# Pooled attention and two MoE layer pairs: another order in the prelude, and the second pair's first operands made in slots of the last token block

## The chip, the cores and the metric

The kernel runs on one core of a Trainium2 chip. The metric is device time in microseconds (us) of that core, as the median of several runs. The engines are TensorE (PE, with its weight loads as PEld), VectorE (DVE), ScalarE (ACT), GpSimd (POOL) and SyncE (SP, which here issues nearly all DMAs).

## The reference

Three stages follow each other on float inputs; weights and inputs of the two layer pairs arrive as float64.

```python
k_p = k.reshape(B, H, Sp, 8, D).mean(axis=3)      # B, H, S, D = 8, 8, 576, 64; Sp = 72
v_p = v.reshape(B, H, Sp, 8, D).mean(axis=3)
scores = scale * np.matmul(q, k_p.transpose(0, 1, 3, 2))
attn = np.exp(scores - np.max(scores, axis=-1, keepdims=True))
attn = attn / (np.sum(attn, axis=-1, keepdims=True) + 1e-09)
x = np.matmul(attn, v_p)                           # then (B*S, H*D) = 4608 x 512
y = ((x @ w_a) * (x @ w_b)) @ w_out                # w_a, w_b 512 x 1536
h = y @ w_in                                       # 512 x 2048
out = (h * np.clip(h + 3.0, 0.0, 6.0) / 6.0) @ w_out2
```

## The kernel before

**Attention.** The tokens are cut into chunks of up to 128, four of them (chunks 0 to 3) in the first block. For a batch, `k_dma` and `k_prep` load k and sum it in eights, `k_write` transposes it on PE (PSUM tile `ktp`) into the block matrix `bd`; `v_prep` and `v_write` make `vmh` and `vml` (the high part of v and the rest) for the first 64 pooled rows; `vl_dma`, `vl_prep`, `vl_split` and `vl_write` do it for the 8 left over (`vlraw`, `vls`, `vlhl`, `vlw`). For a chunk, `q_tr` transposes q (for batch 0 on PE, `qtp`), `scores` makes products `sc` and on DVE their maximum and difference (L263, L264), `expo` the exponential on ACT, `sums` the row sums on DVE (L279 to L283), `normal` the normalised weights on POOL, `at_main` and `at_left` their transposes (`atm`, `atl` on PE) with a split in high and low part (L330, L331, L341, L343), and `pv` the product with v, which fills the token block `xh`, `xl`.

**First layer pair.** There are nine blocks of 512 tokens (NB) and 12 slices of the inner width (NF1). `step(j, f)` makes `pa` and `pb` (from the block and a weight slice; in block 0 four matmuls of 512 columns each, which the trace shows as eight, and later twelve), copies them out on ACT (`asb`, `bsb`), multiplies them on POOL (L689), splits the product into `gh` and `gl`, and issues the `y` products of the step before (`y_part`, four banks), whose result `y_store` copies through the buffers `io` (two of them, tile `yo`) to `ydram`. In block 0 the weights are decoded from float64: `w1_begin` on ACT, `w1_mid` as two operations on DVE and one on POOL (L85 to L87), `w1_end` on DVE (L91), three parts to a slice, and products take one matmul per tile (L505, L519). From block 1 on each product is three matmuls (L497 to L499) of high and low parts.

**Order.** All of this stands in a manually scheduled stretch, in which every engine issues in the order of the code. `prelude()` is written out by hand: it does batch 0's attention for the first block and decodes the first weights. The rest of the attention is cut into pieces that `at(slot, ...)` puts into numbered slots, three to a step (36 to a block), which `run_slot` runs between `pa`, `pb` and `y`. `k_write` stands one slot behind `k_prep`.

**Second layer pair.** It stands behind the manual stretch, where the framework's scheduler picks the order on each engine and may put work ahead of the code's place. Two blocks make a super, and seven products per pair of slices (`in_prod`, banks `phZ`, `phW`, `phX`) work on sums of blocks and of weights. Their first operands are made by `y_load` (four tiles `yb` from `ydram`), `y_pre` (sums `T1`, `T2` and another, on POOL), `s_make` (seven pairs `Sh` on ACT and `Sl`, five of these on DVE and numbers 6 and 3 on POOL; number 4 begins with a sum on DVE), `w2_load` and `w2_make` (four weight sums on POOL, then splits `wi` and `wo` on ACT and DVE, of `wi` numbers 1 and 3 on POOL). A part of the results passes through `hs`, a tile of the same two `io` buffers. In the order that resulted, the first `phW` products stood in the middle of step 8's `y` products of the last block.

Of the kernel before, what the change touches and what calls it, by code (L numbers as in the profile page):

```python
# [8 lines left out]
F32 = mybir.dt.float32  # L9
# [16 lines left out]
def pooled_attention_then_two_moe_kernel(  # L26
# [371 lines left out]
    for c, (b, t0, n) in enumerate(chunks):  # L398
# [177 lines left out]
    def prelude():  # L576

        k_dma(0, 0)
        q_dma(0)
        for hp in range(1, NP):  # L580
            k_dma(0, hp)
# [3 lines left out]
        vl_dma(0)  # L585
        q_dma(2)
        q_dma(3)
        for f in range(3):
            w1_dma(f)
# [4 lines left out]
        def sc(c):  # L594
            q_tr(c)
# [6 lines left out]

        sc(0)
# [105 lines left out]
    with tc.manual_schedule():  # L709
        prelude()  # L710
        for j in range(NB):
            for f in range(NF1):
                step(j, f)
        y_part(*pend)
        y_store(NB - 1, 1)
        for dst, src in later:
            nc.sync.dma_start(dst, src)
        assert not plan and not w2st
    attn_stack.close()
# [5 lines left out]

    p2 = ctx.enter_context(tc.tile_pool(name="p2", bufs=1))
# [11 lines left out]
    def yt_tile(shape, name):  # L738
        return p2.tile(shape, F32, tag="yt", name=name, bufs=6)
# [20 lines left out]
    def w2_make(p):  # L760
        w, o = win_t.pop(p), wout_t.pop(p)
        sums = yt_tile([P, 4, 256], "sums")
        a11, a12, a21, a22 = w[:, 0, 0:256], w[:, 0, 256:512], w[:, 1, 0:256], w[:, 1, 256:512]
        nc.gpsimd.tensor_tensor(sums[:, 1], a21, a22, ALU.add)
        nc.gpsimd.tensor_tensor(sums[:, 2], a11, a21, ALU.subtract)
        nc.gpsimd.tensor_tensor(sums[:, 0], sums[:, 1], a11, ALU.subtract)
        nc.gpsimd.tensor_tensor(sums[:, 3], a12, sums[:, 0], ALU.subtract)
# [7 lines left out]
        for i, sc in enumerate(srcs):  # L775
            t = wpool.tile([P, 4, 256], F32R, tag="w", name=f"wi0_{p}_{i}")
            n = 2 if i < 3 else 1
            split(t[:, 0:n], t[:, n : 2 * n], sc, lo_eng=nc.vector if i % 2 == 0 else nc.gpsimd)
            nc.sync.dma_start(wsd[p][i][:, : 2 * n], t.bitcast(F32)[:, : 2 * n])
            wi_t[0, p].append(t)  # L780
        wo_t[0, p] = []
        for i in range(2):
# [29 lines left out]
    def s_make(s, i):  # L812
# [7 lines left out]
        split(h[:, :, :n], lo[:, :, :n], src, lo_eng=nc.gpsimd if i in (6, 3) else nc.vector)  # L820
        S[s, i] = (h, lo)
# [3 lines left out]
    def g_make(s, p, fi, h, src):  # L825
# [4 lines left out]
        g = p2.tile([P, 2, TB], F32R, tag="g", name="g", bufs=8)  # L830
# [24 lines left out]
    def in_prod(s, p, i):  # L855
# [10 lines left out]
        sh, sl = S[s, i]  # L866
# [28 lines left out]

    y_load(0)
    y_pre(0, 0)
    y_pre(0, 1)
    for i in ORDER:
        s_make(0, i)  # L900
    w2_load(0, 0)
    w2_make(0)
# [56 lines left out]
```

## Time and profile before

| what | value |
|---|---|
| median of three runs | 1855.47 us (1854.78 to 1855.57) |
| profiled execution, its own time | 1853.53 us |
| its span, first to last instruction | 1851.7 us |
| busy share of the span: PE, PEld, DVE, ACT, POOL | 97%, 78%, 51%, 39%, 41% |
| matmuls on PE | 8148 |
| mean granted clock of PE | 0.989 |

The profiled execution's own time is 1.83 us above its span. In the rows below a name is that of a tile, `out<-in` says what an instruction writes and reads, and brackets hold the idle time of the engine ahead of it with what ended that.

### The profile page before, as it was taken

How to read it: one execution, taken by the hardware profiler on the slowest of the kernel's cores; microseconds unless marked ns; L12 is line 12 of the kernel's file. 1: busy time of each engine (PE TensorE's matmuls, PEld its weight loads, DVE VectorE, ACT ScalarE, POOL GpSimd, SP SyncE). 2: the span in 40 equal slices, each digit the busy share in tenths (PEclk: the TensorE clock that was granted, in tenths of full speed). 3: DMA queues.
4: the chain of work that ended last, by engine and by line, in shares of the span. 5: the costliest groups of instructions: out<-in, count | busy, mean ns of one | idle time of the engine just before them, and what ended most of it. 6: DMA issues, size and time to landing. Idle time of an engine off the chain costs nothing.

```text
span 1851.7 us, 23399 instructions
## 1 busy us (share of the span) xinstructions
PE 1796.2 (97%) x8148; PEld 1438.6 (78%) x8148; DVE 947.3 (51%) x1609; ACT 726.9 (39%) x1389; POOL 763.0 (41%) x661
## 2 busy tenths in 40 slices
PE   4999999999999999999999989999999999999998
PEld 3444788888888788888888777888888888888897
DVE  6687655323444445444322336676557445644645
ACT  3544443323333333333333335444334433533443
POOL 3454454333443444444343575554225222422322
PEclk8999999999999999999999999999999999999999
DMA  9552346635746547565545465546445544644483
GB/s 250 174 161 50 115 145 214 217 109 154 247 150 195 199 150 229 183 210 185 187 160 199 163 244 185 207 173 227 151 151 182 178 146 142 210 137 149 152 296 127
DMA packets 196549, 328.72 MB, mean 178 GB/s; under 512 B 86352, under 2 KB 107856, under 8 KB 196432
## 3 DMA queue, kind: packets, MB, share of 16 engines
q1 hardware_dynamic: 196432, 327.22, 53.5%
q8 instruction: 65, 1.06, 0.2%
q14 instruction: 52, 0.43, 0.1%
HBM read 264.24 MB, written 62.91 MB: 177 GB/s over the span
## 4 chain that ended last, share of the span: by engine, by line
PE 88%; DVE 5%; DMA 1%; ACT 1%; issue 1%; POOL 0%; SPq 0%; DVEq 0%; ACTq 0%; POOLq 0%
PE o L497 7%; PE o L499 7%; PE o L498 7%; PE y L497 5%; PE pb L497 5%; PE y L499 4%; PE pb L499 4%; PE y L498 4%; PE pb L498 4%; PE pa L497 4%; PE pa L499 4%; PE pa L498 4%; PE phZ L497 3%; PE phZ L498 3%; PE phZ L499 3%; PE sc L258 2%
## 5 line engine op out<-in xcount | busy, mean ns | idle before, releaser
L74 POOL TENSOR_TENSOR g<-r,g 128x512 fp32r<-128x512 f32 (+1 forms) x160 | 198.3, 1249 | 433.4 <-ACT g L73 263.8
L847 DVE TENSOR_TENSOR oacc<-o,oacc 128x512 f32<-128x512 f32 x252 | 172.2, 688 | 135.7 <-PE o L499 135.5
L498 PE MATMUL o<-wo,g 128*128 128x512 f32 x576 | 224.4, 390 | 0.0
L499 PE MATMUL o<-wo,g 128*128 128x512 f32 x576 | 224.2, 389 | 0.0
L689 POOL TENSOR_TENSOR asb<-asb,bsb 128x512 f32<-128x512 f32 x96 | 126.9, 1322 | 232.1 <-ACT bsb L684 206.8
L497 PE MATMUL o<-wo,g 128*128 128x512 f32 x576 | 211.6, 390 | 1.4 <-ACT g L73 1.2
L74 POOL TENSOR_TENSOR gl<-asb,gh 128x512 fp32r<-128x512 f32 x96 | 126.8, 1321 | 146.3 <-ACT gh L73 144.1
L671 ACT COPY asb<-pa 128x512 f32<-128x512 f32 x108 | 63.3, 586 | 243.0 <-PE pa L499 207.1
L497 PE MATMUL pa<-xh,wa 128*128 128x512 f32 x384 | 154.7, 403 | 0.0
L499 PE MATMUL pa<-xl,wa 128*128 128x512 f32 x384 | 150.2, 391 | 0.0
L498 PE MATMUL pa<-xh,wa 128*128 128x512 f32 x384 | 149.7, 390 | 0.0
L684 ACT COPY bsb<-pb 128x512 f32<-128x512 f32 x108 | 63.3, 586 | 192.4 <-PE pb L499 160.7
L828 ACT ACTIVATE r<-hs 128x512 f32<-128x512 f32 (+1 forms) x120 | 69.0, 590 | 164.7 <-DVE hs L878 163.8
L497 PEld LDWEIGHTS o<-wo,g 128*128 128x128 f32 x576 | 107.5, 188 | 23.8 <-ACT g L73 2.4
L499 PEld LDWEIGHTS o<-wo,g 128*128 128x128 f32 x576 | 108.1, 188 | 22.2
L498 PEld LDWEIGHTS o<-wo,g 128*128 128x128 f32 x576 | 108.2, 188 | 22.0
L73 ACT CAST g<-r 128x512 fp32r<-128x512 f32 (+1 forms) x160 | 91.9, 579 | 68.4 <-DVE r L829 68.2
L498 PE MATMUL phZ<-Sh,wi 128*128 128x512 f32 (+1 forms) x320 | 117.7, 368 | 0.0
L497 PE MATMUL phZ<-Sh,wi 128*128 128x512 f32 (+1 forms) x320 | 117.6, 368 | 0.0
L499 PE MATMUL phZ<-Sl,wi 128*128 128x512 f32 (+1 forms) x320 | 114.6, 368 | 0.0
L331 DVE TENSOR_TENSOR atl<-atm,ath 128x512 fp32r<-128x512 f32 (+1 forms) x40 | 25.5, 637 | 165.6 <-ACT ath L330 165.5
L829 DVE SCALAR_TENSOR_TENSOR r<-r,hs 128x512 f32<-128x512 f32 (+1 forms) x120 | 95.0, 808 | 26.5 <-ACT r L828 26.4
(1349 smaller groups left out, 4216.3 us busy)
## 6 DMA issues: line engine op xcount, KB each, us to landing
wi<-wsd SPq DMA_DIRECT2D x96, 512.0 KB
wo<-wod SPq DMA_DIRECT2D x64, 512.0 KB
wsd<-wi SPq DMA_DIRECT2D x24, 512.0 KB
kraw<-in_k_dram SPq DMA_DIRECT2D x32, 288.0 KB
ydram<-yo SPq DMA_DIRECT2D x36, 256.0 KB
out_dram<-oacc SPq DMA_DIRECT2D x36, 256.0 KB
vraw<-in_v_dram SPq DMA_DIRECT2D x32, 256.0 KB
w2st<-in_moe_w_in_dram SPq DMA_DIRECT2D x16, 512.0 KB
```

What stands on the lines that cost most here:

```text
L73: (hi_eng or nc.scalar.copy)(hi, src)
L74: (lo_eng or nc.gpsimd).tensor_tensor(lo, src, hi.bitcast(F32), ALU.subtract)
L258: nc.tensor.matmul(pt[:n, i * 2 * SP : (i + 1) * 2 * SP], qT[c][:, hp, :], bd[b % 2][hp], start=True, stop=True)
L497: nc.tensor.matmul(o, wh, xh, start=first, stop=False, skip_group_check=more)
L498: nc.tensor.matmul(o, wl, xh, start=False, stop=False, skip_group_check=more)
L499: nc.tensor.matmul(o, wh, xl, start=False, stop=last, skip_group_check=more)
L671: nc.scalar.copy(asb, pa)
L684: nc.scalar.copy(bsb, pb)
L689: nc.gpsimd.tensor_tensor(asb, asb, bsb, ALU.mult)
L828: nc.scalar.activation(r[:, :n], src, AF.Relu, bias=3.0)
L829: nc.vector.scalar_tensor_tensor(r[:, :n], r[:, :n], 6.0, src, ALU.min, ALU.mult)
L847: nc.vector.tensor_tensor(acc, o, acc, ALU.add)
```

## The change

In words:

- In the prelude all four k loads are issued first, then q's chunks 0 and 1, v, q's chunks 2 and 3, and the leftover v last. `q_tr` is called ahead of the scores of an earlier chunk, the scores of the four chunks stand closer together, and the decoding of weights (`w1_begin`, `w1_mid`, `w1_end`) begins behind `normal(3)`. The leftover v of batch 0 is summed on POOL instead of DVE.
- `k_write` of batches 1 and 2 stands two slots behind `k_prep` instead of one.
- The pool `p2` is opened (and the attention's pools closed) at step 6 of the last block instead of behind the manual stretch. Loads, sums and splits for the first super, and pair 0's weights, become a generator, `p2_begin`, advanced by one piece in each slot from step 6 on: 18 slots.
- For the first super `y_pre`, both `Sl` halves that were on POOL, and pair 0's weight sums and `wi` halves go to DVE.

```diff
     def vl_prep(b):
...
-        sum8(vs, t)
+        sum8(vs, t, nc.vector if b else nc.gpsimd)
...
-                at(k_at[hp] + 1, k_write, b, hp)
+                at(k_at[hp] + (2 if b < 3 else 1), k_write, b, hp)
...
     def prelude():
 
-        k_dma(0, 0)
+        for hp in range(NP):
+            k_dma(0, hp)
         q_dma(0)
-        for hp in range(1, NP):
-            k_dma(0, hp)
         q_dma(1)
         v_dma(0, 0)
         v_dma(0, 1)
-        vl_dma(0)
         q_dma(2)
         q_dma(3)
+        vl_dma(0)
...
         def sc(c):
-            q_tr(c)
             scores(c, 0)
             scores(c, 1)
...
+        q_tr(0)
+        q_tr(1)
         sc(0)
         expo(0)
         v_prep(0, 0)
         sc(1)
         sums(0)
+        q_tr(2)
+        expo(1)
         v_prep(0, 1)
-        expo(1)
         normal(0)
-        v_write(0, 0)
+        sc(2)
         sums(1)
-        sc(2)
-        w1_begin(0)
+        q_tr(3)
+        expo(2)
         normal(1)
         at_chunk(0)
-        expo(2)
+        v_write(0, 0)
+        sc(3)
+        sums(2)
+        expo(3)
         vl_prep(0)
+        normal(2)
+        at_chunk(1)
         v_write(0, 1)
-        sums(2)
-        w1_mid(0)
-        sc(3)
-        normal(2)
-        expo(3)
         vl_split(0)
-        at_chunk(1)
-        w1_begin(1)
-        w1_end(0)
+        vl_write(0)
         sums(3)
-        vl_write(0)
         normal(3)
+        w1_begin(0)
         pv(0, 0)
         pv(0, 1)
+        w1_mid(0)
         at_chunk(2)
-        w1_mid(1)
-        w1_begin(2)
+        w1_begin(1)
         at_chunk(3)
-        w1_end(1)
+        w1_end(0)
+        w1_mid(1)
         pv(1, 0)
         pv(1, 1)
+        w1_end(1)
+        w1_begin(2)
         w1_mid(2)
         w1_begin(3)
...
     def w2_make(p):
+
+        pool = nc.gpsimd if p else nc.vector
...
-            split(t[:, 0:n], t[:, n : 2 * n], sc, lo_eng=nc.vector if i % 2 == 0 else nc.gpsimd)
+            split(t[:, 0:n], t[:, n : 2 * n], sc, lo_eng=nc.vector if i % 2 == 0 else pool)
...
     def y_pre(s, i):
         n = supers[s][1]
+        eng = nc.gpsimd if s else nc.vector
...
-        split(h[:, :, :n], lo[:, :, :n], src, lo_eng=nc.gpsimd if i in (6, 3) else nc.vector)
+        split(h[:, :, :n], lo[:, :, :n], src, lo_eng=nc.gpsimd if s and i in (6, 3) else nc.vector)
...
+    P2_AT = 6
+
+    def p2_begin():
+        y_load(0)
+        yield
+        y_pre(0, 0)
+        yield
+        for i in (1, 2):
+            s_make(0, i)
+            yield
+        y_pre(0, 1)
+        yield
+        for i in ORDER[2:]:
+            s_make(0, i)
+            if i == 7:
+                w2_load(0, 0)
+            yield
+        yield from w2_make(0)
+
+    begin2 = p2_begin()
+    for x in range(3 * (NF1 - P2_AT)):
+        at(SLOTS * (NB - 1) + 3 * P2_AT + x, next, begin2, None)
...
+                if j == NB - 1 and f == P2_AT:
+
+                    attn_stack.close()
+                    p2.append(ctx.enter_context(tc.tile_pool(name="p2", bufs=1)))
                 step(j, f)
```

On DVE, this is a piece of the difference in the prelude, from behind the sums of chunk 0 on (`mx`, `sm` are the maxima and differences of a chunk's scores, `su` to `rc` its sums, `atl` and `atx` the split halves of its transposed weights).

```order
+L263 TENSOR_REDUCE mx<-sc 128x4
+L264 TENSOR_TENSOR sm<-sc,mx 128x288
+L263 TENSOR_REDUCE mx<-sc 128x4
+L264 TENSOR_TENSOR sm<-sc,mx 128x288
+L279 TENSOR_REDUCE su<-sm 128x8
+L281 TENSOR_SCALAR se<-su 128x8
+L283 RECIPROCAL rc<-se 128x8
+L331 TENSOR_TENSOR atl<-atm,ath 128x4x128
+L343 TENSOR_TENSOR atx<-atl,atx 32x2x128
 L176 SCALAR_TENSOR_TENSOR vml_108<-vs,vmh_106 64x2x64 x2
-L279 TENSOR_REDUCE su<-sm 128x8
-L281 TENSOR_SCALAR se<-su 128x8
```

The scores of chunk 2 and the sums of chunk 1 now come ahead of `vml`, and the splits of chunk 0 follow them; the sums of `vlraw` and the decoding, which stood further down between these rows, are gone from this stretch.

On PE, this is the difference in the first token block where batch 2's first keys are transposed (`ktp`), behind the products `sc` of an earlier chunk.

```order
-L150 MATMUL ktp<-ident,kp 128x72
-L505 MATMUL pa<-xh_467,rawa_1331 128x512 x4
+L505 MATMUL pa<-xh_509,rawa_1379 128x512 x4
 L340 MATMUL atl<-ident,al 96x64 x2
 L258 MATMUL sc<-bd_2_104,qT 128x144
 L258 MATMUL sc<-bd_3_105,qT 128x144
 L150 MATMUL ktp<-ident,kp 128x72
```

The key transpose that stood directly ahead of a `pa` has moved behind it, and the first one now follows the next products `sc`.

On PE, in the last token block, these are the rows around the first product of the second pair before the change (`y0` to `y3` are the banks of the `y` products; the weights `sp(8, 7)` are those of block 8, slice 7).

```order
L499 MATMUL pb_9290<-xl8_8247,sp(8, 8)_0_9110 128x512
L497 MATMUL y0_8925<-gh_9267,sp(8, 7)_1_9060 128x512
L498 MATMUL y0_8925<-gh_9267,sp(8, 7)_1_9060 128x512
L497 MATMUL phW_9663<-Sh0_2_9559,wi0_0_0_9595 128x512
L498 MATMUL phW_9663<-Sh0_2_9559,wi0_0_0_9595 128x512
L499 MATMUL phW_9663<-Sl0_2_9560,wi0_0_0_9595 128x512
...
L499 MATMUL y0_8925<-gl_9268,sp(8, 7)_1_9060 128x512
L497 MATMUL y1_8926<-gh_9267,sp(8, 7)_1_9060 128x512
L498 MATMUL y1_8926<-gh_9267,sp(8, 7)_1_9060 128x512
```

These are the rows around the same product with the change.

```order
L499 MATMUL pb_9515<-xl8_8295,sp(8, 10)_0_9290 128x512
L497 MATMUL y0_8973<-gh_9488,sp(8, 9)_1_9224 128x512
L498 MATMUL y0_8973<-gh_9488,sp(8, 9)_1_9224 128x512
L497 MATMUL phW_9663<-Sh0_2_9309,wi0_0_0_9460 128x512
L498 MATMUL phW_9663<-Sh0_2_9309,wi0_0_0_9460 128x512
L499 MATMUL phW_9663<-Sl0_2_9310,wi0_0_0_9460 128x512
...
L497 MATMUL phX_9686<-Sh0_5_9369,wi0_0_1_9464 128x512
L498 MATMUL phX_9686<-Sh0_5_9369,wi0_0_1_9464 128x512
L499 MATMUL y0_8973<-gl_9489,sp(8, 9)_1_9224 128x512
L497 MATMUL y1_8974<-gh_9488,sp(8, 9)_1_9224 128x512
```

Before, `phW` stood in the `y` products of slice 7, directly behind `pb` of step 8; now it stands in those of slice 9, behind `pb` of step 10, and two rows of `phX` with it.

On POOL, before, these rows stand in the last block (`yT1`, `yT2` and `yb` are the sums of `y_pre`, `sums` those of pair 0's weights).

```order
L804 TENSOR_TENSOR yT1_9550<-yb_9544,yb_9542 128x1024
L806 TENSOR_TENSOR yT2_9552<-yb_9548,yT1_9550 128x1024
L808 TENSOR_TENSOR yb_9544<-yb_9548,yb_9544 128x1024
L689 TENSOR_TENSOR asb_9237<-asb_9237,bsb_9252 128x512
L74 TENSOR_TENSOR Sl0_6_9564<-yT2_9552,Sh0_6_9563 128x1024
L74 TENSOR_TENSOR Sl0_3_9576<-yb_9548,Sh0_3_9575 128x1024
L764 TENSOR_TENSOR sums_9590<-win_9584 128x256
L765 TENSOR_TENSOR sums_9590<-win_9584 128x256
L74 TENSOR_TENSOR gl_9268<-asb_9237,gh_9267 128x512
L689 TENSOR_TENSOR asb_9288<-asb_9288,bsb_9303 128x512
```

With the change, these rows stand on DVE behind the last decoded weight tile.

```order
L800 TENSOR_TENSOR yT1_9266<-yb_9243,yb_9241 128x1024
L802 TENSOR_TENSOR yT2_9268<-yb_9247,yT1_9266 128x1024
L74 TENSOR_TENSOR Sl0_1_9283<-yb_9241,Sh0_1_9282 128x1024
L74 TENSOR_TENSOR Sl0_2_9310<-yb_9245,Sh0_2_9309 128x1024
L804 TENSOR_TENSOR yb_9243<-yb_9247,yb_9243 128x1024
L74 TENSOR_TENSOR Sl0_6_9343<-yT2_9268,Sh0_6_9342 128x1024
L74 TENSOR_TENSOR Sl0_5_9370<-yT1_9266,Sh0_5_9369 128x1024
L74 TENSOR_TENSOR Sl0_7_9390<-yb_9243,Sh0_7_9389 128x1024
L74 TENSOR_TENSOR Sl0_3_9412<-yb_9247,Sh0_3_9411 128x1024
L806 TENSOR_TENSOR yb_9245<-yb_9245,yT2_9268 128x1024
L74 TENSOR_TENSOR Sl0_4_9436<-yb_9245,Sh0_4_9435 128x1024
L756 TENSOR_TENSOR sums_9455<-win_9393 128x256
```

All sums and halves of the first super now stand together on DVE. On POOL the products `asb` and the halves `gl` of each step remain, and the sums of pair 1's weights come in from the third last product `asb` on.

## Rows read from the trace of the kernel before

**Rows 1.** The page, part 2: granted clock of PE, 40 slices, in tenths.

```profile
PEclk8999999999999999999999999999999999999999
```

**Rows 2.** By windows: stretch, length, busy PE, PEld, DVE, ACT, POOL, clock, DMA.

```profile
0.00:49.61 49.61, 23.80 (x109) 20.48 (x109) 30.77 (x69) 18.83 (x43) 19.13 (x39) 0.79 0.98 253
```

**Rows 3.** Timeline of PE, prelude: start, duration, instruction, [idle before <-releaser].

```profile
38.33 0.58 PE L354 MATMUL pv<-atx,vlw 96*128 96x256 f32 x1 [1.17 <-ACT vlw L205]
...
41.48 1.05 PE L328 MATMUL atm<-ident,am 128*128 128x128 f32 x4
...
49.61 3.60 PE L505 MATMUL pa<-xh,rawa 128*128 128x512 f32 x8
...
69.12 3.70 PE L505 MATMUL pa<-xh,rawa 128*128 128x512 f32 x8 [0.26 <-DVE rawa L91]
```

**Rows 4.** Timeline of SP's DMA issues, prelude.

```profile
7.73 9.22 SPq L182 DMA_DIRECT2D vlraw<-in_v_dram  x6
```

**Rows 5.** Timeline of DVE, prelude: scores, sums and splits.

```profile
16.80 0.46 DVE L263 TENSOR_REDUCE mx<-sc 128x4 f32<-128x288 f32 x1 [3.44 <-PE sc L258]
...
18.25 0.46 DVE L264 TENSOR_TENSOR sm<-sc,mx 128x288 f32<-128x288 f32 x1
...
22.46 0.74 DVE L279 TENSOR_REDUCE su<-sm 128x8 f32<-128x576 f32 x1
...
32.96 0.46 DVE L263 TENSOR_REDUCE mx<-sc 128x4 f32<-128x288 f32 x1
...
46.02 0.42 DVE L343 TENSOR_TENSOR atx<-atl,atx 32x256 fp32r<-32x256 f32 x1
```

**Rows 6.** Timeline of DVE: last step of decoding a weight tile.

```profile
54.15 0.68 DVE L91 SCALAR_TENSOR_TENSOR rawa<-st,rawa 128x512 uint32<-128x512 uint32 x1
...
59.91 0.69 DVE L91 SCALAR_TENSOR_TENSOR raw<-st,raw 128x512 uint32<-128x512 uint32 x1 [2.91 <-POOL raw L87]
...
68.39 0.68 DVE L91 SCALAR_TENSOR_TENSOR rawa<-st,rawa 128x512 uint32<-128x512 uint32 x1
```

**Rows 7.** Timeline of PE, first token block, keys of batch 2.

```profile
172.41 0.38 PE L150 MATMUL ktp<-ident,kp 72*128 72x72 f32 x1 [1.61 <-DVE atl L331]
172.58 5.27 PE L505 MATMUL pa<-xh,rawa 128*128 128x512 f32 x8
```

**Rows 8.** Timeline of PE, last token block and first second-pair product.

```profile
1055.10 0.39 PE L497 MATMUL pa<-xh,wa 128*128 128x512 f32 x1
...
1060.31 0.39 PE L499 MATMUL pb<-xl,sp(8, 8)_0_9110 128*128 128x512 f32 x1
1062.43 0.50 PE L497 MATMUL y<-gh,sp(8, 7)_1_9060 128*128 128x512 f32 x1 [1.74 <-ACT gh L73]
...
1064.87 0.80 PE L497 MATMUL phW<-Sh,wi 128*128 128x512 f32 x1 [1.70 <-ACT wi L73]
1070.58 0.79 PE L498 MATMUL phW<-Sh,wi 128*128 128x512 f32 x1 [4.91 <-DVE wi L74]
...
1072.88 0.63 PE L499 MATMUL y<-gl,sp(8, 7)_1_9060 128*128 128x512 f32 x1
...
1104.08 0.39 PE L497 MATMUL y<-gh,sp(8, 11)_1_9273 128*128 128x512 f32 x1
```

**Rows 9.** Timeline of DVE, last token block: second pair's operands.

```profile
1050.33 1.22 DVE L74 TENSOR_TENSOR Sl<-yb,Sh 128x1024 fp32r<-128x1024 f32 x1 [11.44 <-ACT Sh L73]
...
1057.18 3.42 DVE L810 TENSOR_TENSOR yb<-yb,yT 128x1024 f32<-128x1024 f32 x1 [2.28 <-POOL yT L806]
...
1062.73 6.66 DVE L74 TENSOR_TENSOR Sl<-yb,Sh 128x1024 fp32r<-128x1024 f32 x2
```

**Rows 10.** Timeline of POOL (GpSimd), same stretch.

```profile
1057.11 2.41 POOL L808 TENSOR_TENSOR yb<-yb 128x1024 f32<-128x1024 f32 x1
...
1064.99 3.33 POOL L74 TENSOR_TENSOR Sl<-yb,Sh 128x1024 fp32r<-128x1024 f32 x1
```

**Rows 11.** Timeline of PE, the second product into bank `phW`.

```profile
1114.84 0.79 PE L497 MATMUL phW<-Sh,wi 128*128 128x512 f32 x1 [3.80 <-DVE hs L878]
```

More of the change, by code (lines that the diff above doesn't have):

```diff
@@ L707, in step @@
         pend = (j, f, sp_t.pop(((j, f), 1)), gh, gl)
[L709 to L726, printed above, removed]
+    p2 = []
     NPAIR = NF2 // 2
@@ L738, in yt_tile @@
     def yt_tile(shape, name):
-        return p2.tile(shape, F32, tag="yt", name=name, bufs=6)
+        return p2[0].tile(shape, F32, tag="yt", name=name, bufs=6)
     win_t, wout_t, wi_t, wo_t = {}, {}, {}, {}
@@ L763, in w2_make @@
         a11, a12, a21, a22 = w[:, 0, 0:256], w[:, 0, 256:512], w[:, 1, 0:256], w[:, 1, 256:512]
[L764 to L767, printed above, removed]
+        pool.tensor_tensor(sums[:, 1], a21, a22, ALU.add)
+        pool.tensor_tensor(sums[:, 2], a11, a21, ALU.subtract)
+        pool.tensor_tensor(sums[:, 0], sums[:, 1], a11, ALU.subtract)
+        pool.tensor_tensor(sums[:, 3], a12, sums[:, 0], ALU.subtract)
         wi_t[0, p] = []
@@ L786, in w2_make @@
             wo_t[0, p].append(t)
-    yb, S = {}, {}
+        yield
+    yb, s_ops = {}, {}
     def y_load(s):
@@ L803, in y_pre @@
             yb[s, "T1"] = yt_tile([P, 2, TB], "yT1")
-            nc.gpsimd.tensor_tensor(yb[s, "T1"][:, :, :n], v[0, 1], v[0, 0], ALU.subtract)
+            eng.tensor_tensor(yb[s, "T1"][:, :, :n], v[0, 1], v[0, 0], ALU.subtract)
             yb[s, "T2"] = yt_tile([P, 2, TB], "yT2")
-            nc.gpsimd.tensor_tensor(yb[s, "T2"][:, :, :n], v[1, 1], yb[s, "T1"][:, :, :n], ALU.subtract)
+            eng.tensor_tensor(yb[s, "T2"][:, :, :n], v[1, 1], yb[s, "T1"][:, :, :n], ALU.subtract)
         elif i == 1:
-            nc.gpsimd.tensor_tensor(v[0, 1], v[1, 1], v[0, 1], ALU.subtract)
+            eng.tensor_tensor(v[0, 1], v[1, 1], v[0, 1], ALU.subtract)
         else:
@@ L819, in s_make @@
         lo = wpool.tile([P, 2, TB], F32R, tag="w", name=f"Sl{s}_{i}")
-        split(h[:, :, :n], lo[:, :, :n], src, lo_eng=nc.gpsimd if i in (6, 3) else nc.vector)
-        S[s, i] = (h, lo)
+        split(h[:, :, :n], lo[:, :, :n], src, lo_eng=nc.gpsimd if s and i in (6, 3) else nc.vector)
+        s_ops[s, i] = (h, lo)
     gt, oacc = {}, {}
@@ L829, in g_make @@
         nc.vector.scalar_tensor_tensor(r[:, :n], r[:, :n], 6.0, src, ALU.min, ALU.mult)
-        g = p2.tile([P, 2, TB], F32R, tag="g", name="g", bufs=8)
+        g = p2[0].tile([P, 2, TB], F32R, tag="g", name="g", bufs=8)
         split(g[:, 0, :n], g[:, 1, :n], r[:, :n])
@@ L865, in in_prod @@
         o = zb[bank][:, :n]
-        sh, sl = S[s, i]
+        sh, sl = s_ops[s, i]
         for c in range(2):
@@ L894, in in_prod @@
             g_make(s, p, 1, 0, o)
[L896 to L902, printed above, removed]
+    P2_AT = 6
[8 more added lines that the diff above has]
+        y_pre(0, 1)
+        yield
+        for i in ORDER[2:]:
+            s_make(0, i)
+            if i == 7:
+                w2_load(0, 0)
+            yield
+        yield from w2_make(0)
+    begin2 = p2_begin()
+    for x in range(3 * (NF1 - P2_AT)):
+        at(SLOTS * (NB - 1) + 3 * P2_AT + x, next, begin2, None)
+    with tc.manual_schedule():
+        prelude()
+        for j in range(NB):
+            for f in range(NF1):
+                if j == NB - 1 and f == P2_AT:
+                    attn_stack.close()
+                    p2.append(ctx.enter_context(tc.tile_pool(name="p2", bufs=1)))
+                step(j, f)
+        y_part(*pend)
+        y_store(NB - 1, 1)
+        for dst, src in later:
+            nc.sync.dma_start(dst, src)
+        assert not plan and not w2st
+    for _ in begin2:
+        pass
     prev = []
@@ L909, in pooled_attention_then_two_moe_kernel @@
                 if np_[0] == 0:
-                    w2_make(np_[1])
+                    for _ in w2_make(np_[1]):
+                        pass
             more = s + 1 < len(supers)
```

3 lines of the change are left out of this document (2 added, 1 removed).

## The prediction, made before the changed kernel was run

> **What bounds the kernel now.** I read the page first, for where TensorE (PE) is not at full clock or not busy: its row of granted clock [rows 1] is full except in the first of 40 slices, so what can be won is what PE waits for and the lower clock that follows a wait. The view by windows gives the first stretch: until the first layer-one product PE has 23.80 us of work in 49.61 us, at a granted clock of 0.79, with VectorE (DVE) the busiest engine, 30.77 us [rows 2]. Then PE's timeline, for rows with an idle time in brackets: the prelude [rows 3], a transpose in the middle of the first token block [rows 7], and the end of the last block, where the second pair's first products were put between the last `y` products [rows 8]. DVE's and POOL's (GpSimd's) timelines say what PE waited for there.
>
> **Part 1, the prelude.** Before, DVE handles a chunk's scores in 1.91 us (16.80 to 18.25 + 0.46), but chunk 3's begin only at 32.96 [rows 5]: the decode of weights and `vlraw`'s sums stand ahead of them, and each chunk's q transpose waits its turn. The change puts q transposes one chunk ahead, the four scores close together, and moves `vlraw`'s sums to POOL and the decode to the end.
>
> The start hardly moves. SP's six `vlraw` loads take 9.22 us to issue [rows 4] and now stand behind all of q's; but q's first two loads now stand behind all four k loads, and both must land before the first scores. I give it 0.5 us: DVE begins at 16.3 instead of 16.80.
>
> From there DVE sets the pace. With 1.9 per chunk of scores and 1.1 per chunk of sums (0.74 and two small ones), and an estimate of 1.2 for a chunk's two split subtractions: scores 0 and 1 to 20.1, sums 0 to 21.2, scores 2 to 23.1, sums 1 to 24.2, splits of chunk 0 and the `vml` pair to 26.4, scores 3 to 28.3, sums 2 to 29.4, splits of chunk 1 to 30.6, `vml` and `vlhl` to 31.7. ScalarE's four `vlw` then end near 33.0, and the first `pv` group runs 3.2 us (38.33 to 41.48, where the next transposes start [rows 3]) to 36.2. Before, the last split of chunk 3 ended at 46.44 (46.02 + 0.42 [rows 5]), 4.96 behind that group's end at 41.48; the same lag gives 41.2. Before, the first `pa` came 3.17 behind (49.61 [rows 3]); now near 44.4: **5.2 us earlier**.
>
> Something is late next: decoding. A part is a DVE, POOL, DVE chain of about 3 us, and it now starts after the splits. The fourth part, which the second `pa` needs, ended at 54.83 (54.15 + 0.68 [rows 6]). Now the first part ends near 41.9, the second 3 later, the third near 48.9 behind ScalarE's copies of `xh`, the fourth 4 to 4.5 later (a k sum stands inside it): 53.3, where PE would want it at 51.3. So 2 us are given back for a moment. But before had waits of its own there: the fifth part sat 2.91 for POOL and ended at 60.60, the seventh came 8.5 us later, and `pa` of step 2 waited for it at 69.12 [rows 3, 6]. With the fifth at about 55.9, the seventh comes near 64.4. **I take 4.3 us** at that point; bounds 1.5 (the chain slips by one more part) and 5.5.
>
> **Part 2, `k_write` one slot later for batches 1 and 2.** For batch 2 PE waited 1.61 us at a key transpose for a PSUM buffer, and the next eight matmuls then took 5.27 us [rows 7] instead of 3.60 [rows 3], at the lower clock. Now a `pa` stands between. If both go it is 3.3; the next operands leave a little, so **3.0**. Bounds: 0 (the wait moves to the next row) and 3.3. The slot is still ahead of the scores that read `bd`.
>
> **Part 3, the second pair's first operands.** PE's matmuls of 512 columns start 0.2265 us apart (1055.10 to 1060.31, 23 steps). From the end of the last `pb` of step 8 at 1060.54 to the last `y` group's start at 1104.08 lie 144 matmuls by the program's order: 32.6 us of work in 43.54, so **10.9 us lost**: waits of 1.74, 1.70 and 4.91, and the rest half-clock rows after them (durations 0.79 and 0.63 instead of 0.39) [rows 8]. The first wait is for `gh`, since the product that makes it stood on POOL behind three operand sums; the other two are for `wi_0_0`, whose lower half stood on DVE behind two subtractions that took 6.66 us together beside POOL's of 3.33 [rows 9, 10].
>
> Now y loads, seven S pairs and pair 0's weights are issued from step 6 of the last block on, all on DVE and ScalarE; POOL keeps only two products per step. `phW` moves two steps down, into the `y` products issued in step 10: 74 matmuls after 1060.54, at 1077.3. When is `wi_0_0` ready? At the end of step 9's `pb` (48 matmuls less 24: 1065.98 for `pa`, 1068.7 for `pb`) at most six DVE operations are left: the last S half, four sums, and the half itself. At 1.22 each, the uncollided price of a twice or four times larger operation [rows 9], they end at 1076.0, or earlier. So no wait: **10.9**, bounds 7.5 (a 2 us wait with its half-clock tail) and 12.
>
> The work that hides it is DVE's: a step is 36 matmuls, 8.2 us, and gets about three operations of 1.22. If that cover failed (operations at the collided 3.42 [rows 9]), three are 10.3, more than a step, and `phW` would wait again.
>
> The Trainium skill, Perfetto Trace Analysis, Optimizing Scalar/DVE Operations, speaks against this part: DVE and GpSimd share a read port of SBUF, so moving work between those two might not help. The trace agrees that they hinder each other (1.22 alone, 3.42 beside POOL's 2.41), but not that the move is worthless, since POOL's own time for an equal operand was 3.33 [rows 9, 10]. By the rule alone the 4.9 us wait would stay; by the rows it goes.
>
> A second wait stays. At 1114.84 PE waited 3.80 us for `hs` [rows 11], which needs one of two buffers that the four `yo` copies pass through, two rounds of stores to `ydram`. That chain starts when the last `y` group fills its first bank, some 10 us ahead (1104.08 to 1114.84 [rows 8, 11]), whenever that is, so it moves with the rest: 0.
>
> **The sum.** 4.3 + 3.0 + 10.9 = 18.2. Against the profiled execution's own 1853.53 (span 1851.7) that is 1835.3; that execution lies 1.9 under the median of 1855.47, so the median becomes **1837.3**.
>
> **Rivals.**
> (a) The prelude gives nothing lasting: loads or decoding hold `pa` of step 2 where it was. For it: DVE's first wait is for a load, and decode is a chain. Against: DVE's idle time before 33 is of order, not of data. 18.2 less 4.3, and perhaps 2 more: 1841 to 1844.
> (b) The operands move but `phW` still waits, the rule of the shared port at work: DVE's operations last as at 1057.18. The 4.91 us and a tail of some 2.5 stay: 1844.7. Against it: POOL's long operations are gone from that stretch.
> (c) The second wait shrinks too: with pair 0's stores already gone from SP's queue the `yo` stores leave sooner. It is worth up to 3.80 and its tail, some 5 us: 1832.
> (d) Slower: SP. The four y loads now stand ahead of the last weight loads (`sp` of steps 10 and 11), and the first waits for a buffer that DVE frees. If it is held, `pb` of step 10, due 48 matmuls after 1060.54 at 1071.4, waits for weights. It decides once they are more than 18.2 us late, so with that load held past some 1085. Before, those loads were in by 1050.33, when DVE read them [rows 9], from a place further back in the queue. At 22 us late it would be 1859.
>
> **How the numbers follow.** 0.2% is 3.7 us, about what a measurement of this kernel can tell from no change. My forecast has 0.62 (1832.5 to 1842), (a) 0.12, (b) 0.12, (c) 0.08, (d) 0.03, and 0.03 for something that eats the gain to within 0.2%. So faster 0.94, same 0.03, slower 0.03. The range takes in (a), (b) and most of (c): 1831 to 1846, which leaves out the last two cases and the ends of the bounds.
>
> **What would show it.** Prelude: the first `pa` near 44.4 and chunk 3's scores on DVE near 26.4; wrong if `pa` of step 2 comes after 67. Part 2: no idle time before a key transpose in the first block's last steps and no `pa` of 5.27 after it. Part 3: no wait of PE above 1 us between step 6 of the last block and the last `y` group, DVE's S operations near 1.22, and still a wait of about 4 us before the second `phW`. The prediction is wrong if `phW` waits for `wi_0_0`, or if a load of weights shows in PE's waits.

## The result and the profile after

The changed kernel takes 1838.43 us (median of four runs, 1837.63 to 1838.69) against 1855.41 before (four runs); the ratio is 0.9908, 95% interval 0.9891 to 0.9926, so 13.7 to 20.2 us less. The forecast was 1837.3. The profiled execution took 1837.63 (span 1835.5), 16.2 us less span than before. Where the time went is read at places on PE that both programs pass; the start times come from PE's timelines.

| place on PE | before | after | earlier by | forecast |
|---|---|---|---|---|
| first `pa` | 49.61 | 41.48 | 8.13 | 5.2 |
| `pa` of step 2 | 69.12 | 62.92 | 6.20 | 4.3 |
| first `pa` of block 1 | 198.70 | 189.62 | 9.08 | 7.3 |
| last `y` group | 1104.08 | 1084.15 | 19.93 | 18.2 |
| second `phW` | 1114.84 | 1097.40 | 17.44 | 18.2 |
| end of the span | 1851.7 | 1835.5 | 16.2 | 18.2 |

DVE's timeline of the prelude: the first scores, the scores of chunk 3 and the last split (compare [rows 5]).

```profile
13.75 0.46 DVE L263 TENSOR_REDUCE mx<-sc 128x4 f32<-128x288 f32 x1 [3.44 <-PE sc L258]
...
24.33 0.46 DVE L263 TENSOR_REDUCE mx<-sc 128x4 f32<-128x288 f32 x1
...
37.85 0.42 DVE L343 TENSOR_TENSOR atx<-atl,atx 32x256 fp32r<-32x256 f32 x1
```

The scores begin at 13.75 instead of 16.80, and chunk 3's at 24.33 instead of 32.96. PE's timeline of the first block, its last columns idle time and what ended it (compare [rows 3, 7]):

```profile
41.48 3.65 PE L505 MATMUL pa<-xh,rawa 128*128 128x512 f32 x8
...
49.84 3.67 PE L505 MATMUL pa<-xh,rawa 128*128 128x512 f32 x8 [1.27 <-ACT raw L79]
...
62.92 3.70 PE L505 MATMUL pa<-xh,rawa 128*128 128x512 f32 x8 [1.08 <-DVE rawa L91]
...
164.72 3.67 PE L505 MATMUL pa<-xh,rawa 128*128 128x512 f32 x8 [0.46 <-DVE rawa L91]
...
169.84 0.28 PE L150 MATMUL ktp<-ident,kp 72*128 72x72 f32 x1 [0.52 <-DVE atx L343]
```

PE's first `pa` stands at 41.48, and the next products wait where they waited less or not at all before: 1.27 and 1.08 for decoded weights. The wait of 1.61 ahead of batch 2's key transpose has become 0.46 and 0.52.

PE's timeline of the last block, from the end of step 8's `pb` on (compare [rows 8, 11]):

```profile
1051.29 0.39 PE L499 MATMUL pb<-xl,sp(8, 8)_0_9158 128*128 128x512 f32 x1
...
1068.06 0.39 PE L498 MATMUL y<-gh,sp(8, 9)_1_9224 128*128 128x512 f32 x1
1068.29 0.39 PE L497 MATMUL phW<-Sh,wi 128*128 128x512 f32 x1
...
1084.15 0.39 PE L497 MATMUL y<-gh,sp(8, 11)_1_9352 128*128 128x512 f32 x1
...
1086.65 0.39 PE L499 MATMUL y<-gl,sp(8, 11)_1_9352 128*128 128x512 f32 x1
...
1097.40 0.79 PE L497 MATMUL phW<-Sh,wi 128*128 128x512 f32 x1 [6.28 <-DVE hs L874]
1097.99 0.63 PE L498 MATMUL phW<-Sh,wi 128*128 128x512 f32 x1
```

`phW` follows the `y` product at once, with no idle time, and from 1051.52 (the last `pb` row's start plus its distance of 0.23) to the last `y` group no row waits. The view by windows says the same: stretch, length, busy times of PE, PEld, DVE, ACT and POOL, granted clock, DMA share, GB/s.

```profile
1051.52:1084.15 32.63, 32.63 (x145) 27.02 (x144) 22.57 (x20) 16.88 (x29) 22.03 (x19) 1.00 0.73 269
1084.15:1112.00 27.85, 21.57 (x83) 17.23 (x82) 13.46 (x18) 13.74 (x25) 15.86 (x16) 0.88 0.66 251
```

PE is busy for all of the first 32.63 us at full clock; before, that stretch took 43.54. In the second window lies what was lost again: the second `phW` waits 6.28 us, not 3.80, and then runs at the lower clock.

### The profile page after: what moved, and what is told of

It is laid out like the page before. It is cut to its first block, busy times and chain, and to the rows that moved or that the text cites. A ratio compares the mean times of both kernels' runs of the same rounds, so it can differ in the third digit from the quotient of the medians.

```text
span 1835.5 us, 23397 instructions
## 1 busy us (share of the span) xinstructions
PE 1788.9 (97%) x8148; PEld 1434.7 (78%) x8148; DVE 951.0 (52%) x1617; ACT 727.1 (40%) x1389; POOL 748.0 (41%) x653
## 4 chain that ended last, share of the span: by engine, by line
PE 90%; DVE 5%; DMA 2%; ACT 1%; issue 1%; SPq 0%; POOL 0%; ACTq 0%; DVEq 0%; POOLq 0%
PE o L497 7%; PE o L498 7%; PE o L499 7%; PE pb L497 5%; PE y L497 5%; PE pb L499 5%; PE pb L498 5%; PE y L499 5%; PE y L498 5%; PE pa L497 5%; PE pa L499 5%; PE pa L498 5%; PE phZ L497 3%; PE phZ L498 3%; PE phZ L499 3%; PE sc L258 2%
```

## The experiments

Each run stands beside runs of the kernel before on the same chip. A gain is 1 minus the ratio, times 1855.

**The parts alone.** The first kernel has only the new prelude, with the leftover v's sums on POOL. The edit is the `prelude` part of the diff above.

> The kernel before with the new prelude alone (order, loads, leftover v of batch 0 summed on POOL). Theory: the prelude keeps what the changed kernel shows at the third `pa` (62.92 instead of 69.12), so 6.2 us less: 1849.3. Rival: a part of it is lost again where the old `k_write` slot makes PE wait at batch 2's key transpose, so 3 to 4.5 us less: 1851 to 1852.5.

Measured: 1846.64 (three runs from 1846.34 to 1846.73, one at 1852.12), ratio 0.9958 (0.9942 to 0.9973), so 5.0 to 10.8 us less. PE's timeline:

```profile
41.45 4.40 PE L505 MATMUL pa<-xh,rawa 128*128 128x512 f32 x8
...
63.01 3.70 PE L505 MATMUL pa<-xh,rawa 128*128 128x512 f32 x8 [0.25 <-DVE rawa L91]
```

The `pa` of step 2 is 6.1 us earlier, as in the changed kernel. The theory holds. The old slot's wait at batch 2's key transpose is there, 1.62, but it is no longer than before, so it takes nothing of this gain.

The second kernel has only the slot:

```diff
-                at(k_at[hp] + 1, k_write, b, hp)
+                at(k_at[hp] + (2 if b < 3 else 1), k_write, b, hp)
```

> The kernel before with `k_write` of batches 1 and 2 one slot later, alone. Theory: the wait of 1.61 before the key transpose and the slow `pa` behind it go, 2.9 us less: 1852.6. Rival: without the new prelude the slot makes no difference or costs something in the first steps (batch 1's transposes), 0 to 1 us less: about 1855.

Measured: 1853.83, ratio 0.9988 (0.9979 to 0.9997), 0.6 to 3.9 us less. PE's timeline:

```profile
49.69 4.81 PE L505 MATMUL pa<-xh,rawa 128*128 128x512 f32 x8
...
70.40 3.70 PE L505 MATMUL pa<-xh,rawa 128*128 128x512 f32 x8 [1.08 <-DVE rawa L91]
...
172.19 3.67 PE L505 MATMUL pa<-xh,rawa 128*128 128x512 f32 x8 [0.45 <-DVE rawa L91]
...
177.31 0.28 PE L150 MATMUL ktp<-ident,kp 72*128 72x72 f32 x1 [0.52 <-DVE atx L343]
```

The theory holds where it was meant: at batch 2 the waits fall to 0.45 and 0.52, and from `pa` of step 2 to block 1's first `pa` it takes 126.68 us instead of 129.58, 2.9 less. The rival does not come: from the first `pa` to that of step 2 it takes 20.71 us, before 19.51, but these 1.2 are the first `pa` itself, whose eight matmuls took 4.81 instead of 3.60 [rows 3]. From the `pb` behind it on, the two kernels are 0.01 apart, so the later slot costs nothing at batch 1. In another kernel with the old slot (VectorE left to the scheduler, below) the first `pa` took 5.04 and the same way 20.95.

The third kernel has only the second pair's operands (slots, and DVE instead of POOL), with the old prelude and the old slot of `k_write`.

> The kernel before with the second pair's operands in slots and on DVE, alone. Theory: 10.9 us won up to the last `y` group and about 3.7 lost at the second `phW`, so 7.2 us less: 1848.3, with a wait for `hs` of about 6.3. Rival: the longer wait for `hs` came from the other two parts (or from chance), then 10.9 less: 1844.5, with a wait of about 3.8.

Measured: 1846.73, ratio 0.9950 (0.9936 to 0.9963), 6.9 to 11.9 us less. PE's timeline, the last `y` group and the second `phW`:

```profile
1095.20 0.39 PE L497 MATMUL y<-gh,sp(8, 11)_1_9352 128*128 128x512 f32 x1
...
1108.86 0.79 PE L497 MATMUL phW<-Sh,wi 128*128 128x512 f32 x1 [6.70 <-DVE hs L872]
```

From the end of step 8's `pb` (1062.56) to the `y` group it takes 32.64 us, as in the changed kernel, and the wait for `hs` is 6.70. So both the gain and the longer wait belong to this part. The time, 9.3 us less, lies between the theory's 7.2 and the rival's 10.9 and its interval holds both; it is the wait that speaks against the rival.

**Slots or engine?** Part 3 did two things at once. This kernel keeps the slots and gives the work back to GpSimd:

```diff
-        pool = nc.gpsimd if p else nc.vector
+        pool = nc.gpsimd
...
-        eng = nc.gpsimd if s else nc.vector
+        eng = nc.gpsimd
...
-        split(h[:, :, :n], lo[:, :, :n], src, lo_eng=nc.gpsimd if s and i in (6, 3) else nc.vector)
+        split(h[:, :, :n], lo[:, :, :n], src, lo_eng=nc.gpsimd if i in (6, 3) else nc.vector)
```

> The changed kernel with the second pair's first operands in the same slots, but on GpSimd where they were (sums of blocks and weights, halves 6 and 3, halves 1 and 3 of the weights). Theory: the engine counts, since the halves `gl` of slice 9 queue behind about ten operations on GpSimd; PE waits some 4 to 6 us in the `y` products of slice 9, DVE's operations are stretched, the time is 1843 to 1846. Rival: only the slots count, the move off GpSimd does nothing: no wait above 1 us, 1838.4.

Measured: 1842.56, ratio 0.9931 (0.9915 to 0.9948), about 4 us above the changed kernel. PE's timeline:

```profile
1046.05 0.50 PE L499 MATMUL y<-gl,sp(8, 6)_1_9050 128*128 128x512 f32 x1 [1.51 <-POOL gl L74]
...
1074.19 0.50 PE L499 MATMUL y<-gl,sp(8, 9)_1_9224 128*128 128x512 f32 x1 [0.63 <-POOL gl L74]
...
1103.55 0.79 PE L497 MATMUL phW<-Sh,wi 128*128 128x512 f32 x1 [9.12 <-DVE hs L874]
```

The waits for `gl` are 1.51 and 0.63, less than I expected, and the first `phW` has none. As much again is lost at `hs`, 9.12 instead of 6.28. POOL's timeline shows what held the first `gl`, a block sum of 3.38 us ahead of it and another in between:

```profile
1037.93 3.38 POOL L800 TENSOR_TENSOR yT<-yb 128x1024 f32<-128x1024 f32 x1
...
1043.74 2.25 POOL L74 TENSOR_TENSOR gl<-asb,gh 128x512 fp32r<-128x512 f32 x1
```

The time is just below the expected 1843 to 1846, and half of the loss has another reason than the theory had.

The counterpart is the kernel before (old prelude, old slot) with the work moved to DVE and left behind the manual stretch, to the scheduler (`eng` and `pool` as in the change, no `p2_begin`):

> The kernel before with the second pair's first operands moved from GpSimd to VectorE, but not into slots (the framework's scheduler still places them; it now puts the first `phW` one step later). Theory: the collision of the two engines made 2 of the 3 waits, so moving off GpSimd alone brings 6 to 9 us of the 10.9, with waits of at most 2 us in the transition: 1846 to 1849. Rival: the slots count, since the loads start too late without them; the waits go on with other names: 1852 to 1855.

Measured: 1842.68, ratio 0.9929 (0.9914 to 0.9944), 10.4 to 16.0 us less, past the theory's end. PE's timeline:

```profile
1096.92 0.39 PE L499 MATMUL y<-gl,sp(8, 11)_1_9273 128*128 128x512 f32 x1
...
1101.00 0.50 PE L497 MATMUL phZ<-Sh,wi 128*128 128x512 f32 x1 [0.98 <-ACT kasb L875]
...
1103.83 0.50 PE L497 MATMUL phW<-Sh,wi 128*128 128x512 f32 x1 [1.15 <-DVE hs L880]
```

DVE's timeline shows the price of an operation there and the lower half of `wi_0_0`, and PE's the first `phW`:

```profile
1061.34 1.21 DVE L74 TENSOR_TENSOR Sl<-yb,Sh 128x1024 fp32r<-128x1024 f32 x1
...
1066.85 0.68 DVE L74 TENSOR_TENSOR wi<-win,wi 128x512 fp32r<-128x512 f32 x1
```

```profile
1068.44 0.39 PE L497 MATMUL phW<-Sh,wi 128*128 128x512 f32 x1
```

The waits at `phW` are gone without any slot, and that for `hs` is 1.15. But this is not the engine alone: the scheduler also put the first `phW` one step later, into the `y` products of slice 8. The half that it needs ends at 1067.53, 0.9 ahead of it; at the old place, behind the first two `y` rows of slice 7 at 1060.28, it would have waited some 7 us (an estimate from these rows). How much of the gain is the engine and how much this later place was not tried apart.

The four kernels make a square; the first number is the stretch from the end of step 7's `pb` to the end of the last `y` product, 192 matmuls in three of them and 198 in the slots on GpSimd, whose six more (1.36) are taken off. Of each, 43.5 is work.

| | left to the scheduler | in slots |
|---|---|---|
| GpSimd | 54.42, wait for `hs` 3.80 (before) | 46.27, wait 9.12 |
| VectorE | 45.48, wait 1.15 | 43.52, wait 6.28 (changed kernel) |

Either edit ends most of what was lost in the stretch, 8.2 and 8.9 of 10.9 us, so they are substitutes and not parts of a sum. At the second wait they differ: the slots lengthen it by some 5 us, the engine shortens it by some 3. On balance the slots cost time: beside the third kernel, which has slots and VectorE, this one takes 2.0 us more in the stretch, but 741.88 instead of 748.71 from the last `y` product to the end of the span. The times point the same way (13.2 against 9.3 us less), though their intervals overlap.

**The second wait.** This kernel takes `hs` from another tag, whose two buffers are idle there:

```diff
-            d = spool.tile([P, TB], F32, tag="io", name="hs")
+            d = spool.tile([P, TB], F32, tag="wst", name="hs")
```

> The changed kernel with `hs` in the two buffers of another tag that lie idle there, so that it shares none with `yo`. Theory: the second `phW` waits for nothing but these buffers; its wait of 6.28 and the half-clock rows behind it (12 rows at 0.43 instead of 0.23, 2.5 us) go: 8 to 9 us less than the changed kernel, about 1830. Rival: the stores' traffic holds PE up anyway (weights, `wo` or `g` come late as well), then under 4 us less: above 1834.

Measured: 1830.29, ratio 0.9861 (0.9848 to 0.9875), 8 to 9 us under the changed kernel. PE's timeline, all waits above 0.3 us there:

```profile
1095.67 0.49 PE L497 MATMUL phZ<-Sh,wi 128*128 128x512 f32 x1 [0.57 <-DVE hs L874]
...
1099.22 0.50 PE L497 MATMUL phW<-Sh,wi 128*128 128x512 f32 x1 [0.52 <-DVE hs L874]
```

The theory holds: from the last `y` product to the end of the span it takes 741.48 us instead of 748.85, 7.4 less. With other buffers the scheduler also orders some products otherwise, so a part of it may be the order.

This one lets ScalarE issue the last block's stores:

```diff
-            nc.sync.dma_start(ydram[j][:, c], yo)
+            (nc.scalar if j == NB - 1 else nc.sync).dma_start(ydram[j][:, c], yo)
```

> The changed kernel with the four stores of `yo` of the last block issued by ScalarE instead of SyncE, whose queue has the second pair's loads and stores of weights ahead of them. Theory: the longer wait for `hs` (6.28 instead of 3.80) is that queue: the first store left 2.08 us after its copy ended; with it gone the wait falls to about 3.5 to 4, and the time to 1835 to 1836. Rival: the stores land later because the memory traffic is denser (251 GB/s instead of 215 in this stretch), then the wait stays near 6 and the time at 1838.4.

Measured: 1834.07, ratio 0.9887 (0.9873 to 0.9902). This interval and the changed kernel's overlap a little; the traces tell the two apart, with 745.22 us instead of 748.85 from the last `y` product to the end. PE's order is the same as in the changed kernel. First SP's timeline of the changed kernel, then ACT's of this one with its issues (ACTq):

```profile
1084.06 3.55 SPq L771 DMA_DIRECT2D wsd<-wi  x2
1087.70 1.21 SPq L533 DMA_DIRECT2D ydram<-yo  x2
```

```profile
1085.77 0.59 ACT L530 COPY yo<-y 128x512 f32<-128x512 f32 x1 [1.03 <-PE y L499]
1086.39 1.11 ACTq L533 DMA_DIRECT2D ydram<-yo  x2
```

In the changed kernel the first copy ends at 1085.62 (ACT, 1085.03 plus 0.59) and its store is issued at 1087.70, 2.08 later, behind two stores of weights that hold SP for 3.55. Here it is issued at 1086.39, 0.03 after the copy. PE's wait is 4.26:

```profile
1096.11 0.80 PE L497 MATMUL phW<-Sh,wi 128*128 128x512 f32 x1 [4.26 <-DVE hs L874]
```

So 2.0 of the 2.5 us by which the wait had grown are SP's queue (in three other runs with these slots and SP the wait is 6.66 to 6.97, in three others with the old operands 3.77 to 4.65). The rest shows in the second round of stores: from the issue of its first store to `hs` it is 4.74 here (1090.62 to 1095.36) and 4.46 in the changed kernel (1092.19 to 1096.65), before 3.45 (1110.64 to 1114.09). The rival's denser traffic would fit that, 367 GB/s from 1084 to 1097 in the changed kernel against 255 from 1104 to 1115 before, but it was not tried.

**The prelude.** The old order of loads in the changed kernel:

```diff
-        for hp in range(NP):
-            k_dma(0, hp)
+        k_dma(0, 0)
         q_dma(0)
+        for hp in range(1, NP):
+            k_dma(0, hp)
         q_dma(1)
         v_dma(0, 0)
         v_dma(0, 1)
+        vl_dma(0)
         q_dma(2)
         q_dma(3)
-        vl_dma(0)
```

> The changed kernel with the loads of the prelude in the old order. Theory: the new order of loads is what brought DVE's first scores from 16.80 to 13.75 (all four k sums run without a wait for a load); without it the first scores are near 16.8, and the first `pa` comes 2.5 to 3 us later than 41.48, of which some 2 us last: about 1840.5. Rival: q's transposes ahead of time brought it, then the first scores stay under 14.5 and the time at 1838.4.

Measured: 1842.98, ratio 0.9935 (0.9920 to 0.9950). PE's timeline:

```profile
46.02 3.60 PE L505 MATMUL pa<-xh,rawa 128*128 128x512 f32 x8
...
67.77 3.70 PE L505 MATMUL pa<-xh,rawa 128*128 128x512 f32 x8 [1.07 <-DVE rawa L91]
```

DVE's first scores come at 18.45, the first `pa` 4.5 us later, and all of it lasts. That is more than I expected. The transposes one chunk ahead are not the reason: in 11 of the 14 profiles, old and new order alike, the first scores start 4.98 us behind the start of the last k sum, and in the other three 4.99 to 5.09. Here that sum starts at 13.47, since the k sums wait 3.62, 0.23 and 0.91 for loads; before, it starts at 11.82, and with the operands alone, where the loads have the same old order, at 12.81. So k's loads landed later in this execution; why is open.

The reverse, the new order of loads in the kernel before:

> The kernel before with the new order of loads in the prelude alone. Theory: the loads gave about 4.5 us of the 8.1 by which the first `pa` came earlier (the old order in the changed kernel lost 4.5), and give the same alone, since DVE's k sums run without waits: first `pa` near 45.5, 1851 to 1852. Rival: without the transposes ahead of time the earlier k is of no use, since the order on DVE holds the chunks anyway: 1854 to 1855.5.

Measured: 1854.64, ratio 0.9997 (0.9987 to 1.0006), no difference. PE's timeline:

```profile
47.17 4.09 PE L505 MATMUL pa<-xh,rawa 128*128 128x512 f32 x8
...
67.16 3.70 PE L505 MATMUL pa<-xh,rawa 128*128 128x512 f32 x8 [0.26 <-DVE rawa L91]
```

DVE's first scores come at 13.96 instead of 16.80, the first `pa` is 2.4 us earlier and `pa` of step 2 2.0; but the end of the span is not. In this run the stretch from step 8's `pb` to the last `y` group takes 45.8 us instead of 43.5, with a first wait of 2.60 instead of 1.74, and takes the gain back. Neither number of the theory came out in the time, and whether that loss repeats is open.

The leftover v's sums back on DVE (`sum8(vs, t)`):

> The changed kernel with the leftover v of batch 0 summed on DVE as before (three operations, 1.4 us together). Theory: DVE sets the pace of the prelude, so the first `pa` comes 1.4 us later, near 42.9, and about 1 us lasts: 1839.4. Rival: DVE has idle time ahead of the last splits (2.49 us at 35.29), so the sums fit in and nothing changes: 1838.4.

Measured: 1839.51, ratio 0.9918 (0.9903 to 0.9932). PE's timeline has the first `pa` at 42.84, 1.36 later, and `pa` of step 2 at 64.58, 1.66 later; the time is 1.1 above the changed kernel. Of the 1.36, 0.36 are there at the first scores already (14.11 instead of 13.75), so about 1.0 is the sums'. That fits the theory in kind, while the times alone do not tell it from none.

**Put together.** `hs` in its own buffers, and `k_write` two slots behind for all batches (`k_at[hp] + 2`):

> The changed kernel with `hs` in its own two buffers and `k_write` two slots behind `k_prep` for all batches. Theory: 8 us from `hs`, and the six waits of 0.3 to 1.1 at key transposes of batches 3 to 7 (4.5 us together) go with their slow rows: 1825 to 1827. Rival: these waits only move to the next row: 1830.

Measured: 1828.64, ratio 0.9856 (0.9842 to 0.9871). Of the waits meant, 0.68 at 545 and one of 0.91 are gone, the others stay, as in these rows of PE's timeline:

```profile
305.90 0.28 PE L150 MATMUL ktp<-ident,kp 72*128 72x72 f32 x1 [1.12 <-DVE atx L343]
...
684.86 0.28 PE L150 MATMUL ktp<-ident,kp 72*128 72x72 f32 x1 [0.91 <-DVE xl L360]
```

These waits end with other work on DVE (`atx`, `xl`), one slot later as well; I read it as a PSUM bank that this work frees. The 1.7 us to the run with `hs` alone lie inside the intervals, but PE's timelines show a gain: from block 1's first `pa` to the end of step 8's `pb` in the last block it takes 859.30 us here and 859.39 in the next run, against 861.58 to 861.79 in eleven profiles with the old slot from batch 3 on. So the slot is worth 2.3 us there, half of the theory's 4.5.

The last adds `w1_begin(2)` and `w1_mid(2)` ahead of the second `pv` group:

```diff
         at_chunk(3)
+        w1_begin(2)
         w1_end(0)
         w1_mid(1)
+        w1_mid(2)
+        w1_end(1)
         pv(1, 0)
         pv(1, 1)
-        w1_end(1)
-        w1_begin(2)
-        w1_mid(2)
         w1_begin(3)
```

> As the one before, and the third weight part of the prelude begun ahead of the second `pv` group instead of behind it. Theory: after the first `pa` the chain of decoding sets the pace (waits of 1.27, 0.98 and 1.08 at the next three products), and 1.3 to 2 us of it go: 1.3 to 2 us under the one before. Rival: ScalarE's copies of `xh` are held up by it and the first `pa` comes as much later: the same.

Measured: 1827.78, ratio 0.9848 (0.9832 to 0.9865), the fastest of all, but not told apart from the one before. PE's timeline:

```profile
49.20 3.60 PE L505 MATMUL pa<-xh,rawa 128*128 128x512 f32 x8
...
62.04 3.70 PE L505 MATMUL pa<-xh,rawa 128*128 128x512 f32 x8 [1.08 <-DVE rawa L91]
...
103.78 5.37 PE L505 MATMUL pb<-xh,raw 128*128 128x512 f32 x8 [0.42 <-DVE raw L91]
```

The second `pa` no longer waits: it follows the first by 7.01 us, in the eight other profiles with the new prelude's order by 8.35 to 8.68 (in the run just before, no wait shows either, since its first `pa` took 5.13). From DVE's first scores (14.36, and 13.82 in the run before) to `pa` of step 2 it takes 47.68 us instead of 49.00, so 1.3 were won there; the prelude's scores began 0.5 later in this execution, and a `pb` fell to the lower clock (below).

## Why the prediction was right, step by step

**The start of the prelude was mis-sized.** "The start hardly moves ... I give it 0.5 us": it moved 3.05. I had looked at q's loads moving back and not at k's. Before, DVE's k sums waited 2.05, 0.69 and 0.46 for loads; with all four k loads ahead of q none of these waits is left. **The rest of that chain held.** From the first to chunk 3's scores I had 10.1 us, measured 10.58; from the first scores to the first `pa` 28.1, measured 27.73. So 2.55 of the 2.9 us by which the first `pa` beat the forecast are the loads. Both runs on the loads show it: with the old ones the scores come at 18.45, with the new ones alone at 13.96, and there the first `pa` moves 2.4.

**Decoding as the next thing late** was right in kind: of 8.13, 6.20 are left at `pa` of step 2, so 1.93 are given back where I had 0.9. The waits are for the parts that I named, and the last run shows it, since an earlier third part takes the second `pa`'s wait away. The 6.20 itself is one pair of executions: `pa` of step 2 stands at 69.12 to 70.99 in four profiles with the old prelude and at 62.32 to 63.53 in six with the new one, so it could have been measured as anything from 5.6 to 8.7.

**Part 2 came out**, 2.88 (9.08 less 6.20) against 3.0, and, as its two terms had it, it hangs on the clock. From the start of the `pb` near 110 to block 1's first `pa` it is 87.93 before and 84.97 after. With the old slot the wait of 1.60 to 1.62 is there in all five profiles, but the eight matmuls behind it took 5.27 to 5.34 us in three and 3.64 or 3.65 in the other two, where the stretch is 86.17 and 85.84. So the slot is worth 0.9 us where the clock stays up and some 2.6 where it falls, and the 3.0 came out because the clock fell in the profile that I forecast from. My sign for this part, no idle time before a key transpose, did not come quite: 0.52 is left. With the new slot the waits are 0.44 to 0.52 and no row behind them was slow, in nine profiles of nine.

**Part 3 was right to the number and half right in its reason.** The stretch went from 43.54 to 32.63, 10.91. The lower half of `wi_0_0` ends at 1065.19 (1063.97 plus 1.22, DVE's timeline), 3.1 ahead of `phW`.

```profile
1043.60 1.22 DVE L804 TENSOR_TENSOR yb<-yb 128x1024 f32<-128x1024 f32 x1
...
1055.87 2.31 DVE L806 TENSOR_TENSOR yb<-yb,yT 128x1024 f32<-128x1024 f32 x1
...
1063.97 1.22 DVE L74 TENSOR_TENSOR wi<-win,wi 128x512 fp32r<-128x512 f32 x1
```

An operation takes 1.22, as the forecast had it, and a block sum that falls beside a POOL operation 2.31. But I put the gain down to slots and engine together, and the square shows that each of the two edits ends most of it. The Trainium skill, Perfetto Trace Analysis, Optimizing Scalar/DVE Operations, holds that moving work between DVE and GpSimd might not help since they share a port. Here it helped: that edit alone, with the later place that the scheduler then gave `phW`, was worth 10.4 to 16.0 us. The rows before the change say why moving it can pay: POOL's long operations stood ahead of `gh`'s product and stretched DVE's ([rows 9, 10]).

**"It moves with the rest: 0" was wrong**, by 3.7 us, and with it my sign of a wait of about 4 us: it is 6.28. I took the `yo` chain as a constant of about 10 us. DVE's timeline of the changed kernel shows its rounds:

```profile
1092.36 0.69 DVE L532 COPY yo<-y 128x512 f32<-128x512 f32 x1 [3.35 <-DMA ydram<-yo]
...
1096.65 0.69 DVE L874 TENSOR_TENSOR hs<-phW,kgl 128x512 f32<-128x512 f32 x1 [3.00 <-DMA ydram<-yo]
```

From the first copy on ACT (1085.03) to `hs` it is 11.62 us; before, 9.13 (1104.96 to 1114.09). Two rounds of stores pass through two buffers, and the first store left 2.08 after its copy instead of 1.12. Rival (c) had this with the wrong sign: it expected pair 0's stores to be gone from SP's queue. They were gone before as well, and by the count of these stores it is pair 2's first two that stand ahead of `yo` in both kernels. This is SP's timeline before the change:

```profile
1102.35 4.22 SPq L779 DMA_DIRECT2D wsd<-wi  x2
```

There they begin 2.6 us ahead of the first copy's start (1104.96), with the change 1.0 ahead (1084.06 against 1085.03), so the same queue holds the store longer. Of the 3.73, 2.49 are the wait and 1.24 the rows at the lower clock behind it.

So 4.3 + 3.0 + 10.9 became 6.2 + 2.9 + 10.9, less 3.7: 16.3, and the span fell by 16.2. Two errors of opposite sign kept the total, which is luck: the mechanism of parts 2 and 3 was right, the start of the prelude and the second wait were not. Rivals (a), (b) and (d) did not come: `pa` of step 2 did not stay where it was, `phW` did not wait for `wi_0_0`, and no weight load shows in PE's waits. In (d) the bound does not follow: 1071.4 plus 18.2 is 1089.6, not 1085; nothing hangs on it.

## What to carry to other kernels

Where an edit moves work both in place and to another engine, run each half: here each half alone ended most of the first waits, the new place lengthened another, and by the traces the engine without the slots came out ahead. Where a scheduler orders the rest, look at what it moved as well before the gain is put down to the engine. A wait that ends on a store's landing depends on what the issuing queue holds ahead of that store, so it need not move as a constant when that queue's other work moves; here a buffer of another tag took it away, and another issuing engine shortened it by 2.0 us. The Trainium skill, Perfetto Trace Analysis, DMA Optimizations, says that it may make sense to give loads one issuing engine and stores another. Here, for four stores that stood behind two other stores, another engine was worth some 4 us (1834.07 against 1838.43).

## What the runs showed of the hardware that was not expected

The same idle time is followed by a lower clock in one execution and by none in another. In all 14 profiles a `pb` of block 0 stands behind waits of 1.64 to 1.66 and 0.42 us. Its eight matmuls took 5.29 to 5.37 us in five (before, the prelude alone, the operands alone, the new loads alone, the last run) and 3.67 in nine, with new and old prelude and slot on both sides. What decides it is open. The first `pa`, with no wait shown directly ahead of it, varies as well: 3.60 to 5.13 us for its eight matmuls in 14 profiles. The length of a wait does not decide it either: behind the second `phW`'s wait, 1.6 us were lost to slow rows after 3.80, 2.8 after 6.28 (changed kernel) and 1.7 after 9.12 (slots on GpSimd). The slow `pb` costs little, since the scores' products behind it wait about 1.1 us where it is fast: from the start of this `pb` to block 1's first `pa` it is 85.38 in the last run and 84.96 in the one before.
